# A second expert layer's row blocks are cut anew: seven late pairs, two single blocks and six small blocks in place of eight, one and five

## Chip, cores and metric

The kernel runs on one core of a Trainium2 chip. The metric is the device time in microseconds of one execution of the whole program. Three runs of the kernel before gave 780.1, 777.2 and 779.71 us; their median, 779.71 us, is the time that the change is measured against.

## What is computed

Three layers follow each other, all in float32. The first is a gated linear attention with complex decay over 4 x 8 heads of 768 steps and 48 channels, the second a layer of 3072 rows with a maximum over three products. The third, which the change touches, is a layer with eight experts of which each row takes one:

```python
xn = x / (np.linalg.norm(x, axis=-1, keepdims=True) + 1e-06)
en = expert_emb / (np.linalg.norm(expert_emb, axis=-1, keepdims=True) + 1e-06)
logits = xn @ en.T / tau
expert_idx = np.argmax(logits, axis=1)
...
gate_w = probs[np.arange(N), expert_idx]
for e in range(E):
    mask = expert_idx == e
    h = np.maximum(x[mask] @ w1[e], 0.0)
    out[mask] = gate_w[mask, None] * (h @ w2[e])
```

There are N = 3072 rows of 384, and an expert has a hidden width of 1024. On the inputs drawn here the eight experts take 1305, 521, 427, 153, 107, 15, 14 and 530 rows; of the first 2816 rows 1199 go to expert 0, and no other expert has 512 of them.

## The kernel before

**Stages.** `phase1` (L1073 on) computes the attention and the first dense layer. Its instructions go through a `Recorder`, which plans their order on each engine from written-out costs and then issues them, so that they all carry line L368. At its end `route_early` (L1011) routes the first 22 tiles of 128 rows. `phase2` (L1418) is the expert layer; its instructions carry their own lines, and the order on each engine is set by the scheduler of the tile framework from modelled times.

**Blocks of rows.** Rows of one expert are gathered from the DRAM tensor `x1d` by indirect loads into blocks of 128 (`gather`, L1264), and a block's result is scattered to `out` in the same manner (L1358). There are three kinds of step:
- A pair is two blocks, 256 rows, of one expert. Its products are made of float32r halves: weights and rows are split into a high and a low part and three products are added. The first product takes 72 matmuls (L1336), the second 24 for each block (L1352).
- A single is one block. Its first product is plain float32 (`ph<-xT,w1s` in the trace, 48 records), its second is as in a pair.
- A small block, or mini (`small`, L1362), holds up to MT = 32 rows of one expert. It loads its expert's two weights for itself (`w1m` and `w2m`, 1.5 MB each, one buffer each), and its few matmuls (`pxm`, `phm`, `pt`, `pym`, `psm`) are placed between those of one step and the next.

**How rests are cut.** `late_route` (L1157) counts the rows of every expert, takes off the early pairs, and calls `pairs_of` with a least of 129: a rest of 129 to 256 rows is a pair with empty places. What is then left is a mini if it has up to 32 rows, else single blocks. With the counts above that is: four early pairs of expert 0; eight late pairs (one of expert 0, two of 1, two of 2, one of 3, two of 7); one single (expert 4); five minis (experts 0, 1, 5, 6, 7).

**Order.** `STEPS` lists the steps. Steps 0 and 1 are the first early pair taken as two singles, then come the pairs 2 to 6, the single as step 7, and the pairs 8 to 13. `WITH = 5, 7, 9, 11, 12` are the steps with a mini. Seven further single steps (`SPARE`) are run by `last_blocks` only if the counts need them. In step k the program gathers the rows of step k + 2, loads the weights of step k + 1 (skipped on the chip by `cond` if the expert stays), and splits those weights on ScalarE and VectorE (`prep`, L1288 to L1298). The next mini's first weight and its rows (`xgm`, L1373) are asked for in the step ahead of it; its second weight at its step's start. At most four row buffers (`xg`, `xgm`) live at once.

**Gates.** In both routes `slots` (L968) writes a one-hot table of blocks, multiplied by row number and by three bfloat16 parts of each row's gate (L982 to L991), and `place` (L994) multiplies it on TensorE with one-hot positions. `join` (L1002) adds the parts up, so that `gate_of` holds the gate of every place; the results' last step (`yo`, L1356; `ym`, L1412) multiplies by it. `late_route` runs beside steps 1 to 3.

The lines that set the cut:

```python
TE, PE, PL, SG = 22, 4, 8, E
KE, KP = 2 * PE, 2 * (PE + PL)
NBLK = KP + SG
MT, MINI = 32, 5
SPARE = 7
STEPS = steps("ppppp" "s" "pppppp")
WITH = 5, 7, 9, 11, 12
```

Of the kernel before, what the change touches and what calls it, by code (L numbers as in the profile page):

```python
# [9 lines left out]
F32 = mybir.dt.float32  # L10
F32R = mybir.dt.float32r
BF16 = mybir.dt.bfloat16
# [24 lines left out]

TE, PE, PL, SG = 22, 4, 8, E
KE, KP = 2 * PE, 2 * (PE + PL)
NBLK = KP + SG  # L40
MT, MINI = 32, 5

SPARE = 7


def steps(order):

    out, p, s = [(0, 1), (1, 1)], 2, KP
    for c in order:
        out.append((p, 2) if c == "p" else (s, 1))  # L50
        p, s = (p + 2, s) if c == "p" else (p, s + 1)
    assert (p, s) == (KP, NBLK - SPARE)
    return out + [(i, 1) for i in range(s, NBLK)]


STEPS = steps("ppppp" "s" "pppppp")

WITH = 5, 7, 9, 11, 12
NE, NS = 1 + PE, len(STEPS)

# [322 lines left out]
class Prog:  # L383
# [6 lines left out]
    def consts(self, pool):  # L390
# [46 lines left out]
        self.dst = pool.tile([128, NBLK + MINI - KE], I32, name="dstrow")  # L437
        self.gate_of = pool.tile([128, NBLK + MINI], F32, name="slotgate")

# [515 lines left out]
    def pairs_of(self, new, cnt, T, n, least, name):  # L955

        v = self.q.vector

        k256 = self.k128[:, 1 + (least == 256):min(T + 1, NTILE):2]
        gt, num, tk = new([E, k256.shape[1]], name + "gt"), new([E], name + "n"), new([E], name + "t")  # L960
        v.tensor_tensor(gt, bc(cnt, 2, k256.shape[1]), bc(k256, 1, E), op=ALU.is_ge if least == 256 else ALU.is_gt)
        v.tensor_reduce(num, gt, axis=AX.X, op=ALU.add)
        st, end = self.sums(new, num, name)
        v.tensor_scalar_min(tk, st, float(n))
        v.scalar_tensor_tensor(tk, end, float(n), tk, op0=ALU.min, op1=ALU.subtract)
        return num, st, end, tk

    def slots(self, new, slot1, T, k):  # L968

        v = self.q.vector  # L970
        v.tensor_mul(slot1, slot1, self.oh[:, :, :T])
        slot = new([T], "slot")
        v.tensor_reduce(slot, slot1.rearrange("p e t -> p t e"), axis=AX.X, op=ALU.add)
        v.tensor_scalar_add(slot, slot, -1.0)
        si, pb = new([3, T], "sloti", I32), new([2, T], "posblk")
        v.tensor_copy(si[:, 0], slot)
        v.tensor_scalar(si[:, 1], si[:, 0], 127, None, op0=ALU.bitwise_and)
        v.tensor_scalar(si[:, 2], si[:, 0], 7, None, op0=ALU.arith_shift_right)
        v.tensor_copy(pb, si[:, 1:])

        g, r, gp = self.gates[:, :T], new([T], "grest"), new([T, 4], "gparts", BF16)
        for i in range(3):  # L982
            v.tensor_copy(gp[:, :, i], g)
            if i < 2:
                v.tensor_sub(r, g, gp[:, :, i])
                g = r
        ohb, val = new([T, k], "ohb", BF16), new([T, 5, k], "ohval", BF16)
        v.tensor_tensor(ohb, bc(self.blk[:, :k], 1, T), bc(pb[:, 1], 2, k), op=ALU.is_equal)
        v.tensor_mul(val[:, :, 0], ohb, bc(self.k128[:, :T], 2, k))
        v.tensor_scalar(val[:, :, 1], ohb, self.row1, None, op0=ALU.mult)  # L990
        v.tensor_mul(val[:, :, 2:], bc(ohb, 2, 3), bc(gp[:, :, :3], 3, k))  # L991
        return pb[:, 0], val
# [8 lines left out]

    def join(self, tok, gate, ps):  # L1002
        v = self.q.vector
        ps = ps.rearrange("p (a k) -> p a k", a=5)
        v.tensor_copy(tok, ps[:, 0])
        v.tensor_add(tok, ps[:, 1], tok)
        v.tensor_copy(gate, ps[:, 2])
        for i in (3, 4):
            v.tensor_add(gate, ps[:, i], gate)

    def route_early(self):  # L1011
# [36 lines left out]
        v.scalar_tensor_tensor(rank, rank, 1.0, ok, op0=ALU.add, op1=ALU.mult)  # L1048
        at, val = self.slots(new, rank, T, N)
        ps = self.tl(self.pg, [128, 5 * N], "g", 2, "slots0")  # L1050
# [5 lines left out]
        tok = new([N], "tok")  # L1056
        self.join(tok, self.gate_of[:, :N], ps)
        v.tensor_scalar_add(self.src[:, :N], tok, -1.0)
# [98 lines left out]
    def late_route(self, pool, pg):  # L1157
# [18 lines left out]
        v.tensor_scalar(left, rank, 0.0, None, op0=ALU.is_ge)  # L1176
        _, st, end, tk = self.pairs_of(new, cnt, T, PL, 129, "mid")
        v.tensor_copy(ends[:, 0], end)
# [11 lines left out]
        few, bm = new([E], "few"), new([MINI, E], "bem")  # L1190
        v.tensor_scalar(few, cnt, float(MT), None, op0=ALU.is_le)
        v.tensor_mul(few, few, nb)
        stm, endm = self.sums(new, few, "few")
# [20 lines left out]

        v.tensor_scalar(stm, stm, 128.0, 1.0 + 128 * (NBLK - KE), op0=ALU.mult, op1=ALU.add)
        v.tensor_sub(stm, stm, base[:, 1])
        v.tensor_mul(stm, stm, few)
        v.tensor_add(base[:, 1], base[:, 1], stm)
        s2 = new([E, T], "slot2")
        v.tensor_add(s2, rank, bc(base[:, 1], 2, T))  # L1220
        v.scalar_tensor_tensor(s2, rank, 0.0, s2, op0=ALU.is_ge, op1=ALU.mult)
        v.tensor_add(slot, slot, s2)
        v.tensor_mul(slot, slot, left)
        self.gate(new, lg, mx, self.gates[:, late])
        yield
        at, val = self.slots(new, slot, T, N)
        ps = pg.tile([128, 5 * N], F32, tag="rt", bufs=1, name="slots")
        for t0 in range(0, T, 6):
# [3 lines left out]
        tok, e0 = new([N], "tok"), new([2, N], "empty")  # L1232
        self.join(tok, self.gate_of[:, KE:], ps)
        v.tensor_scalar(e0[:, 0], tok, 1.0, 0.0, op0=ALU.subtract, op1=ALU.max)
# [7 lines left out]
    def moe2(self, pool, wq, pg, regs, q1, q2):  # L1242
# [21 lines left out]
        def gather(i, n):  # L1264
            for i in range(i, i + n):
                xg = pool.tile([128, DM], F32, tag="xg", bufs=4, name=f"xg{i}")
                g.indirect_dma_start(out=xg, out_offset=None, in_=self.x1d[:TE * 128] if i < KE else self.x1d,
                                     in_offset=bass.IndirectOffsetOnAxis(ap=self.src[:, i:i + 1], axis=0),
                                     bounds_check=(TE * 128 if i < KE else NT) - 1, oob_is_err=False)
                st["x", i] = xg  # L1270

        def prep(i, n):
# [71 lines left out]
        def mm2(i, n, b):  # L1344
            py = pg.tile([128, DM], F32, tag="py", bufs=2, name=f"py{i}_{b}")
            w2, o, m = st["w2", i], 0, 4 // n
            r = slice(b * 128, (b + 1) * 128)
            for k in range(KF):
                (hi, lo), (wh, wl) = st["h", i, k // 4, k % 4 // m], w2[k // 4]
                f = k % m  # L1350
                for a, c in ((hi, wh), (hi, wl), (lo, wh)):
                    t.matmul(py, a[:, f, r], c[:, k % 4], start=o == 0, stop=o == 3 * KF - 1)  # L1352
                    o += 1
            i += b
            y = pool.tile([128, DM], F32, tag="yo", bufs=3, name=f"yo{i}")
            s.activation(y, py, AF.Copy, scale=self.gate_of[:, i:i + 1])  # L1356
            row = self.src[:, i:i + 1] if i < KE else self.dst[:, i - KE:i - KE + 1]
            g.indirect_dma_start(out=self.io["out"], in_=y, in_offset=None,  # L1358
                                 out_offset=bass.IndirectOffsetOnAxis(ap=row, axis=0), bounds_check=NT - 1, oob_is_err=False)
        return load, gather, prep, share, transpose, mm1, mm2, st  # L1360

    def small(self, pool, mp, pg, m):  # L1362
# [11 lines left out]
                             in_offset=bass.IndirectOffsetOnAxis(ap=self.src[:, i:i + 1], axis=0),  # L1374
                             bounds_check=NT - 1, oob_is_err=False)
        yield

# [33 lines left out]
        y = pool.tile([128, DM], F32, tag="yo", bufs=3, name=f"ym{m}")  # L1411
        s.activation(y, ps, AF.Copy, scale=self.gate_of[:, i:i + 1])  # L1412
        g.indirect_dma_start(out=self.io["out"], in_=y, in_offset=None,
# [85 lines left out]
    def run(self):  # L1499
        tc = self.tc  # L1500
        with ExitStack() as ctx:
# [6 lines left out]
            self.x1d = dp.tile([NT, DM], F32, name="x1d")  # L1508
            self.xd = dp.tile([NT, DM], F32, name="xd")
            self.phase1()  # L1510
            self.phase2()
# [38 lines left out]
    def last_blocks(self):  # L1550
# [3 lines left out]
        with self.tc.tile_pool(name="lb", bufs=1) as p, self.tc.tile_pool(name="lbg", bufs=1, space=PSUM) as pg, \  # L1554
# [6 lines left out]
            nc.sync.dma_start(dst, self.dst[:, bass.ds(k + (i0 - KE), 1)])  # L1561
            nc.sync.dma_start(gate, self.gate_of[:, bass.ds(k + i0, 1)])
            e = nc.values_load(tab[0:1, :], engines=[ET.SP], min_val=0, max_val=E - 1,
                               skip_runtime_bounds_check_because="a count of 8 comparisons, of which one fails")
            w1 = p.tile([128, 3, FF2], F32, name="lb_w1")
            w2 = p.tile([128, FF2 // 128, DM], F32, name="lb_w2")
# [220 lines left out]
```

## Time and profile before

| | us |
|---|---|
| median of three runs (777.2 to 780.1) | 779.71 |
| profiled execution, device time | 777.83 |
| its span, first to last instruction | 775.9 |
| TensorE busy with matmuls | 719.6 (93% of the span) |
| VectorE busy | 607.1 (78%) |
| ScalarE busy | 441.5 (57%) |
| GpSimd busy | 104.6 (13%) |

The span leaves 1.9 us of the device time outside it. Matmuls are pipelined, so TensorE counts as busy almost without a break where nothing stops it; what a step costs there is read from the distance between the starts of its first and the next step's first matmul. "Idle before" is the time in which an engine had nothing running ahead of an instruction, with what ended it. The granted clock is given as a share of full speed.

### The profile page before, as it was taken

To read this page: it belongs to the slowest core of one execution; us is meant where nothing else is said; L and a number is where in the kernel's file an instruction comes from. 1 tells how busy PE (TensorE), PEld (TensorE's weight loads), DVE (VectorE), ACT (ScalarE), POOL (GpSimd) and SP (SyncE) were. 2 spreads that over 40 slices of the span, in tenths; PEclk is the share of its full clock that TensorE was granted. 3 is DMA by queue.
4 is the path that set the end of the run, shared out by engine and by line. 5 is a ranking of instruction groups with operands and counts; after the bars stand their busy time and mean duration, and the time that the engine had idled before them with its cause. 6 is when DMAs were issued, how large, how long until landed. Compare 5 with 4: busy or idle time off the path is not lost. (4 is left out here: it accounts for less than half of the span.)

```text
span 775.9 us, 18425 instructions
## 1 busy us (share of the span) xinstructions
PE 719.6 (93%) x7318; PEld 657.1 (85%) x7318; DVE 607.1 (78%) x1211; ACT 441.5 (57%) x1007; POOL 104.6 (13%) x156
## 2 busy tenths in 40 slices
PE   0568989999999999999999999999999999999995
PEld 0447679899899989888998988989989898999985
DVE  8999799999999999999999722869986455546420
ACT  8997485656667555757455442167535466544521
POOL 6301000000000000000000000022122223324211
PEclk9987899999999999999999999999999999999999
DMA  8608062635345380834516240051058775691500
GB/s 330 263 21 197 1 174 69 139 131 137 106 105 119 91 209 13 197 99 119 137 37 140 60 86 22 13 233 42 22 236 335 283 299 213 210 368 49 186 22 26
DMA packets 28753, 107.42 MB, mean 138 GB/s; under 512 B 5061, under 2 KB 8180, under 8 KB 25569
## 3 DMA queue, kind: packets, MB, share of 16 engines
q1 hardware_dynamic: 20432, 77.55, 33.5%
q0 software_dynamic: 7952, 28.21, 11.3%
q8 instruction: 59, 0.97, 0.5%
q10 hardware_dynamic: 272, 0.39, 0.1%
q14 instruction: 38, 0.30, 0.1%
HBM read 96.35 MB, written 10.62 MB: 138 GB/s over the span
## 5 line engine op out<-in xcount | busy, mean ns | idle before, releaser
L368 PE MATMUL ph<-xhi,w 128*128 128x256 f32 x864 | 134.0, 291 | 0.9 <-ACT xhi L368 0.9
L368 PEld LDWEIGHTS ph<-xhi,w 128*128 128x128 f32 x864 | 114.3, 191 | 8.3 <-issue 4.7
L1298 DVE TENSOR_TENSOR w2l<-queue_q_buf,w2h 128x768 fp32r<-128x768 f32 x52 | 47.9, 954 | 39.1 <-ACT w2h L1297 39.0
L1336 PE MATMUL ph<-xh,w1s 128*128 128x256 f32 x264 | 77.0, 292 | 0.0
L368 PE MATMUL ph<-xlo,w 128*128 128x256 f32 x432 | 75.3, 283 | 0.4 <-DVE xlo L368 0.4
L1336 PE MATMUL ph<-xh,w1l 128*128 128x256 f32 x264 | 74.6, 283 | 0.0
L1336 PE MATMUL ph<-xl,w1s 128*128 128x256 f32 x264 | 74.6, 283 | 0.0
L1352 PE MATMUL py<-w2h,hlo 128*128 128x384 f32 x200 | 67.9, 340 | 1.8 <-DVE hlo L1341 1.8
L1352 PE MATMUL py<-w2h,hhi 128*128 128x384 f32 x200 | 69.1, 345 | 0.0
L1352 PE MATMUL py<-w2l,hhi 128*128 128x384 f32 x200 | 67.6, 338 | 0.0
L368 PEld LDWEIGHTS ph<-xlo,w 128*128 128x128 f32 x432 | 62.0, 191 | 0.6 <-DVE xlo L368 0.6
L368 POOL DMA_DIRECT2D v<-v x24 | 12.9, 538 | 365.4 <-PE py L368 364.5
L1341 DVE SCALAR_TENSOR_TENSOR hlo<-ph,hhi 128x512 fp32r<-128x512 f32 x50 | 34.3, 688 | 30.0 <-ACT hhi L1340 30.0
L1340 ACT ACTIVATE hhi<-ph 128x512 fp32r<-128x512 f32 x50 | 29.9, 598 | 49.0 <-PE ph L1336 48.8
L368 PE MATMUL pa<-S 112*128 112x128 f32 x384 | 51.7, 279 | 2.2 <-DVE at L368 1.7
L1336 PEld LDWEIGHTS ph<-xh,w1s 128*128 128x128 f32 x264 | 50.5, 191 | 3.8 <-issue 3.1
L368 PEld LDWEIGHTS pa<-S 112*128 112x128 f32 x384 | 48.2, 193 | 4.5 <-DVE at L368 2.9
L1297 ACT CAST w2h<-queue_q_buf 128x768 fp32r x52 | 40.8, 833 | 18.1 <-PE py L1352 16.7
L1336 PEld LDWEIGHTS ph<-xh,w1l 128*128 128x128 f32 x264 | 50.5, 191 | 0.5
L1336 PEld LDWEIGHTS ph<-xl,w1s 128*128 128x128 f32 x264 | 50.5, 191 | 0.0
L368 DVE TENSOR_TENSOR sa<-X 128x384 f32<-128x384 f32 x84 | 46.5, 554 | 0.7
L1292 DVE TENSOR_TENSOR w1l<-queue_q_buf,w1s 128x1536 fp32r<-128x1536 f32 x22 | 38.6, 1759 | 9.3 <-PE ph L1336 7.4
(399 smaller groups left out, 1809.1 us busy)
## 6 DMA issues: line engine op xcount, KB each, us to landing
queue_q_buf<-w SPq DMA_DIRECT2D x26, 1536.0 KB
S<-QK SPq DMA_DIRECT2D x46, 289.1 KB
X<-a SPq DMA_DIRECT2D x11, 768.0 KB
QKr<-qk SPq DMA_DIRECT2D x11, 768.0 KB
w1m<-w SPq DMA_DIRECT2D x5, 1536.0 KB
w2m<-w SPq DMA_DIRECT2D x5, 1536.0 KB
v<-v POOLq DMA_DIRECT2D x24, 224.0 KB, 3.6
r<-w POOLq DMA_DIRECT2D x12, 384.0 KB, 8.4
```

What stands on the lines that cost most here:

```text
L368: getattr(getattr(self.nc, c[0]), c[1])(*c[2], **c[3])
L1292: v.tensor_sub(wl[k], av.rearrange("p (a b) -> p a b", b=FF2)[:, :, c], w1[k].bitcast(F32))
L1297: s.copy(hi, b[:, c])
L1298: v.tensor_sub(lo, bv[:, c], hi.bitcast(F32))
L1336: t.matmul(ph[:, f], a, b, start=o == 0, stop=o == len(ops) - 1)
L1340: s.activation(hi, ph, AF.Relu).ins,
L1341: v.scalar_tensor_tensor(lo, ph, 0.0, hi.bitcast(F32), op0=ALU.max, op1=ALU.subtract).ins]
L1352: t.matmul(py, a[:, f, r], c[:, k % 4], start=o == 0, stop=o == 3 * KF - 1)
```

## The change

The limit from which a rest becomes a pair is raised from 129 to 161 rows. Rests of 129 to 160 rows become one single block and one mini, for which `late_route` tells an expert's last, small block from its full ones (`s3`). With the counts above, expert 3's 153 rows are no longer a pair but a single of 128 and a mini of 25. There are seven late pairs, two singles (experts 3 and 4) and six minis. The singles are the last two steps, 12 and 13, and the minis lie in steps 6 to 11, all of them pairs.

The late gates are no longer placed by matmuls: all gates are turned by one transposition on TensorE, copied by ScalarE, and written to a DRAM tensor `gd`. For each late block and each mini the GpSimd queue issues one more indirect load, of 128 single gates, right behind that of its rows (`gate_rows`, six buffers). In `slots` the product with the row number in the tile moves from VectorE to ScalarE, in the early route too.

```diff
-TE, PE, PL, SG = 22, 4, 8, E
+TE, PE, PL, SG = 22, 4, 7, E + 2
-MT, MINI = 32, 5
-SPARE = 7
+MT, MINI = 32, 6
+SPARE = 8
-STEPS = steps("ppppp" "s" "pppppp")
-WITH = 5, 7, 9, 11, 12
+STEPS = steps("ppppppppppss")
+WITH = 6, 7, 8, 9, 10, 11
...
-    def slots(self, new, slot1, T, k):
+    def slots(self, new, slot1, T, k, parts):
...
-        g, r, gp = self.gates[:, :T], new([T], "grest"), new([T, 4], "gparts", BF16)
-        for i in range(3):
-            v.tensor_copy(gp[:, :, i], g)
-            if i < 2:
-                v.tensor_sub(r, g, gp[:, :, i])
-                g = r
-        ohb, val = new([T, k], "ohb", BF16), new([T, 5, k], "ohval", BF16)
+        ohb, val = new([T, k], "ohb", BF16), new([T, 2 + parts, k], "ohval", BF16)
         v.tensor_tensor(ohb, bc(self.blk[:, :k], 1, T), bc(pb[:, 1], 2, k), op=ALU.is_equal)
+        self.q.scalar.activation(val[:, :, 1], ohb, AF.Copy, scale=self.row1)
         v.tensor_mul(val[:, :, 0], ohb, bc(self.k128[:, :T], 2, k))
-        v.tensor_scalar(val[:, :, 1], ohb, self.row1, None, op0=ALU.mult)
-        v.tensor_mul(val[:, :, 2:], bc(ohb, 2, 3), bc(gp[:, :, :3], 3, k))
+        if parts:
...
-        _, st, end, tk = self.pairs_of(new, cnt, T, PL, 129, "mid")
+        _, st, end, tk = self.pairs_of(new, cnt, T, PL, 128 + MT + 1, "mid")
...
-        v.tensor_scalar(few, cnt, float(MT), None, op0=ALU.is_le)
-        v.tensor_mul(few, few, nb)
+        v.scalar_tensor_tensor(few, nb, -128.0, cnt, op0=ALU.mult, op1=ALU.add)
+        v.tensor_scalar(few, few, float(MT - 128), None, op0=ALU.is_le)
+        v.scalar_tensor_tensor(few, nb, 1.0, few, op0=ALU.min, op1=ALU.mult)
...
+        v.tensor_scalar_mul(nb, nb, 128.0)
         v.tensor_sub(stm, stm, base[:, 1])
+        v.tensor_sub(stm, stm, nb)
         v.tensor_mul(stm, stm, few)
-        v.tensor_add(base[:, 1], base[:, 1], stm)
-        s2 = new([E, T], "slot2")
-        v.tensor_add(s2, rank, bc(base[:, 1], 2, T))
+        s2, s3 = new([E, T], "slot2"), new([E, T], "slot3")
+        v.tensor_tensor(s3, rank, bc(nb, 2, T), op=ALU.is_ge)
+        v.tensor_mul(s3, s3, bc(stm, 2, T))
+        v.tensor_add(s3, s3, bc(base[:, 1], 2, T))
+        v.tensor_add(s2, s3, rank)
...
         self.gate(new, lg, mx, self.gates[:, late])
+        pt, rows = pg.tile([T, 128], F32, tag="rt", bufs=1, name="pgate"), pool.tile([T, 128], F32, name="grow")
+        t.transpose(pt, self.gates, self.ident)
+        self.q.scalar.copy(rows.rearrange("t (b l) -> t l b", l=L), pt.rearrange("t (l b) -> t l b", l=L))
+        self.q.sync.dma_start(self.gd.rearrange("(t p) a -> t (p a)", p=128), rows)
         yield
-        at, val = self.slots(new, slot, T, N)
-        ps = pg.tile([128, 5 * N], F32, tag="rt", bufs=1, name="slots")
+        at, val = self.slots(new, slot, T, N, 0)
+        ps = pg.tile([128, 2 * N], F32, tag="rt", bufs=1, name="slots")
...
-        self.join(tok, self.gate_of[:, KE:], ps)
+        self.join(tok, ps)
...
                 st["x", i] = xg
+                if i >= KE:
+                    st["gate", i] = self.gate_rows(pool, i)
...
-            s.activation(y, py, AF.Copy, scale=self.gate_of[:, i:i + 1])
+            s.activation(y, py, AF.Copy, scale=self.gate_of[:, i:i + 1] if i < KE else st.pop(("gate", i)))
...
+    def gate_rows(self, pool, i):
+
+        x = pool.tile([128, 1], F32, tag="grow", bufs=6, name=f"gate{i}")
+        self.nc.gpsimd.indirect_dma_start(out=x, out_offset=None, in_=self.gd,
+                                          in_offset=bass.IndirectOffsetOnAxis(ap=self.src[:, i:i + 1], axis=0),
+                                          bounds_check=NT - 1, oob_is_err=False)
+        return x
```

The mini's `small` calls `gate_rows` behind its own gather and scales `ym` by it. `join` leaves the gates out where none are given, `gate_of` keeps the eight early blocks only, `pairs_of` compares with the remainder of the least, and `last_blocks` loads its gates from `gd`.

## Rows read from the trace of the kernel before

**Rows 1.** The page: the span; VectorE and the granted clock in 40 slices.

```profile
span 775.9 us, 18425 instructions
...
DVE  8999799999999999999999722869986455546420
...
PEclk9987899999999999999999999999999999999999
```

**Rows 2.** Two windows: length, busy PE, PEld, DVE, ACT, POOL, clock, DMA share, GB/s.

```profile
534.93:576.66 41.73, 39.94 (x283) 38.82 (x282) 40.80 (x114) 19.79 (x28) 8.63 (x6) 0.96 0.20 77
594.05:768.04 173.99, 173.15 (x1313) 159.69 (x1312) 83.57 (x98) 85.00 (x130) 45.53 (x39) 1.00 0.51 192
```

**Rows 3.** Windows of four steps of the second MoE, same columns.

```profile
576.66:594.05 17.39, 17.39 (x126) 17.39 (x126) 9.80 (x13) 9.98 (x14) 5.08 (x5) 1.00 1.01 412
...
634.38:646.80 12.42, 12.42 (x108) 11.35 (x108) 6.21 (x9) 8.70 (x13) 5.04 (x5) 1.00 0.45 162
...
688.20:706.56 18.36, 18.36 (x133) 18.09 (x129) 9.87 (x12) 9.66 (x15) 5.06 (x5) 1.00 0.62 246
...
728.00:750.18 22.18, 22.18 (x177) 19.41 (x173) 10.93 (x13) 8.82 (x16) 3.28 (x4) 1.00 0.23 85
```

**Rows 4.** Groups of PE instructions by line and shape, 500 to 776 us.

```profile
L1336 PE MATMUL ph<-xT,w1s 128*128 128x128 f32 x144 | 16.7, 276 | 0.0
...
L1390 PE MATMUL phm<-w1m,xm 128*32 128x256 f32 x120 | 7.5, 383 | 0.0
...
L999 PE MATMUL slots<-ohval,ohpos 128*128 128x145 bf16 x24 | 2.3, 229 | 0.0
```

**Rows 5.** VectorE in order of time, 530 to 570 us: start, length, line.

```profile
536.96 0.27 DVE L983 CAST gparts<-gates 128x24 bf16<-128x24 f32 x1
...
545.37 0.17 DVE L1192 TENSOR_TENSOR few<-few,nblocks 128x8 f32<-128x8 f32 x1
...
551.90 0.36 DVE L1220 TENSOR_TENSOR slot<-incl,base 128x192 f32<-128x192 f32 x1
...
563.62 0.41 DVE L990 TENSOR_SCALAR ohval<-ohb,row 128x696 bf16<-128x696 bf16 x1
563.93 2.33 DVE L991 TENSOR_TENSOR ohval<-ohb,gparts 128x2088 bf16<-128x2088 bf16 x1
```

**Rows 6.** TensorE in order of time, 568 to 573 us.

```profile
568.92 0.57 PE L999 MATMUL slots<-ohval,ohpos 128*128 128x145 bf16 x6
571.28 0.44 PE L1352 MATMUL py<-w2h,hlo 128*128 128x384 f32 x1 [1.79 <-DVE hlo L1341]
...
572.50 0.52 PE L1352 MATMUL py<-w2l,hhi 128*128 128x384 f32 x1
```

**Rows 7.** GpSimd queue in order of time, 590 to 592 us.

```profile
590.08 1.00 POOL L1358 DMA_INDIRECT out<-yo,srcrow  x1 [10.85 <-DMA out<-yo,srcrow]
591.38 1.04 POOL L1373 DMA_INDIRECT xgm<-x1d,srcrow  x1 [0.30 <-issue]
```

**Rows 8.** TensorE in order of time, 597 to 600 us.

```profile
599.35 0.34 PE L1383 MATMUL pxm<-ident,xgm 32*128 32x32 f32 x3 [0.84 <-DMA xgm<-x1d,srcrow]
```

**Rows 9.** GpSimd queue in order of time, 718 to 728 us.

```profile
718.01 1.02 POOL L1373 DMA_INDIRECT xgm<-x1d,srcrow  x1 [4.40 <-PE pxg L1313]
...
727.59 1.00 POOL L1358 DMA_INDIRECT out<-yo,dstrow  x1 [2.63 <-ACT yo L1356]
```

**Rows 10.** TensorE in order of time, 733 to 734 us.

```profile
733.14 0.37 PE L1383 MATMUL pxm<-ident,xgm 32*128 32x32 f32 x3
```

**Rows 11.** Instructions that touch xgm: GpSimd durations min/median/max, DMA to landing.

```profile
L1373 POOL DMA_INDIRECT xgm<-x1d,srcrow x5: 998/1040/1992, 591.4 to 718.0; - x5
...
DMA to landing us min/median/max: 3.8/8.7/10.3
```

**Rows 12.** Instructions that touch xg, 500 to 777 us.

```profile
L1267 POOL DMA_INDIRECT xg<-x1d,srcrow x24: 994/1022/2558, 503.8 to 711.6; - x24
```

**Rows 13.** One wait of TensorE over the span: total us, times, longest.

```profile
PE pk L368 <- DMA S<-QK: 2.1, 2, 1.6
```

More of the change, by code (lines that the diff above doesn't have):

```diff
@@ L437, in consts @@
         self.dst = pool.tile([128, NBLK + MINI - KE], I32, name="dstrow")
-        self.gate_of = pool.tile([128, NBLK + MINI], F32, name="slotgate")
+        self.gate_of = pool.tile([128, KE], F32, name="slotgate")
         self.mtab = pool.tile([128, MINI], I32, name="mtab")
@@ L960, in pairs_of @@
         gt, num, tk = new([E, k256.shape[1]], name + "gt"), new([E], name + "n"), new([E], name + "t")
-        v.tensor_tensor(gt, bc(cnt, 2, k256.shape[1]), bc(k256, 1, E), op=ALU.is_ge if least == 256 else ALU.is_gt)
+        v.scalar_tensor_tensor(gt, bc(cnt, 2, k256.shape[1]), float(least % 128), bc(k256, 1, E), op0=ALU.subtract,
+                               op1=ALU.is_ge)
         v.tensor_reduce(num, gt, axis=AX.X, op=ALU.add)
@@ L979, in slots @@
         v.tensor_copy(pb, si[:, 1:])
-        g, r, gp = self.gates[:, :T], new([T], "grest"), new([T, 4], "gparts", BF16)
-        for i in range(3):
-            v.tensor_copy(gp[:, :, i], g)
-            if i < 2:
-                v.tensor_sub(r, g, gp[:, :, i])
-                g = r
-        ohb, val = new([T, k], "ohb", BF16), new([T, 5, k], "ohval", BF16)
+        ohb, val = new([T, k], "ohb", BF16), new([T, 2 + parts, k], "ohval", BF16)
         v.tensor_tensor(ohb, bc(self.blk[:, :k], 1, T), bc(pb[:, 1], 2, k), op=ALU.is_equal)
+        self.q.scalar.activation(val[:, :, 1], ohb, AF.Copy, scale=self.row1)
         v.tensor_mul(val[:, :, 0], ohb, bc(self.k128[:, :T], 2, k))
-        v.tensor_scalar(val[:, :, 1], ohb, self.row1, None, op0=ALU.mult)
-        v.tensor_mul(val[:, :, 2:], bc(ohb, 2, 3), bc(gp[:, :, :3], 3, k))
+        if parts:
+            g, r, gp = self.gates[:, :T], new([T], "grest"), new([T, 4], "gparts", BF16)
+            for i in range(3):
+                v.tensor_copy(gp[:, :, i], g)
+                if i < 2:
+                    v.tensor_sub(r, g, gp[:, :, i])
+                    g = r
+            v.tensor_mul(val[:, :, 2:], bc(ohb, 2, 3), bc(gp[:, :, :3], 3, k))
         return pb[:, 0], val
@@ L1000, in place, with join @@
                                      stop=t0 + k == T - 1)
-    def join(self, tok, gate, ps):
+    def join(self, tok, ps, gate=None):
         v = self.q.vector
-        ps = ps.rearrange("p (a k) -> p a k", a=5)
+        ps = ps.rearrange("p (a k) -> p a k", k=tok.shape[1])
         v.tensor_copy(tok, ps[:, 0])
         v.tensor_add(tok, ps[:, 1], tok)
+        if gate is None:
+            return
         v.tensor_copy(gate, ps[:, 2])
@@ L1048, in route_early @@
         v.scalar_tensor_tensor(rank, rank, 1.0, ok, op0=ALU.add, op1=ALU.mult)
-        at, val = self.slots(new, rank, T, N)
+        at, val = self.slots(new, rank, T, N, 3)
         ps = self.tl(self.pg, [128, 5 * N], "g", 2, "slots0")
@@ L1056, in route_early @@
         tok = new([N], "tok")
-        self.join(tok, self.gate_of[:, :N], ps)
+        self.join(tok, ps, self.gate_of)
         v.tensor_scalar_add(self.src[:, :N], tok, -1.0)
@@ L1375, in small @@
                              bounds_check=NT - 1, oob_is_err=False)
+        gate = self.gate_rows(pool, i)
         yield
@@ L1411, in small @@
         y = pool.tile([128, DM], F32, tag="yo", bufs=3, name=f"ym{m}")
-        s.activation(y, ps, AF.Copy, scale=self.gate_of[:, i:i + 1])
+        s.activation(y, ps, AF.Copy, scale=gate)
         g.indirect_dma_start(out=self.io["out"], in_=y, in_offset=None,
@@ L1509, in run @@
             self.xd = dp.tile([NT, DM], F32, name="xd")
+            self.gd = dp.tile([NT, 1], F32, name="gd")
             self.phase1()
@@ L1561, in last_blocks @@
             nc.sync.dma_start(dst, self.dst[:, bass.ds(k + (i0 - KE), 1)])
-            nc.sync.dma_start(gate, self.gate_of[:, bass.ds(k + i0, 1)])
             e = nc.values_load(tab[0:1, :], engines=[ET.SP], min_val=0, max_val=E - 1,
                                skip_runtime_bounds_check_because="a count of 8 comparisons, of which one fails")
+            nc.gpsimd.indirect_dma_start(out=gate, out_offset=None, in_=self.gd,
+                                         in_offset=bass.IndirectOffsetOnAxis(ap=src, axis=0),
+                                         bounds_check=NT - 1, oob_is_err=False)
             w1 = p.tile([128, 3, FF2], F32, name="lb_w1")
```

## The prediction, made before the change ran

> **What bounds the kernel now.** I read the page first [rows 1]: VectorE is near full only in the first half and around two thirds of the span, and TensorE has its full clock but for the start and one later dip. The change touches the expert layer, so I cut its stretch into windows [rows 2]. Two things are to be seen. From 594 us to the last matmul TensorE is busy 173.15 of 173.99 us, VectorE 83.57, ScalarE 85.00, GpSimd 45.53, and the DMA has a share of 0.51: there every matmul taken out is time gained. In the 41.73 us from 534.93 on VectorE is busy 40.80, TensorE idles 1.79 us, and the mean clock is 0.96: there VectorE, which carries the late routing beside the splitting of weights, sets the pace. Windows of single steps [rows 3] then give the prices.
>
> **The exchange of blocks.** A pair goes; a single and a mini come.
> - The pair: the window from 688.20 holds one without a mini, 18.36 us, but also the sum of the mini before it. That from 576.66 has none, 17.39 us, but starts two of its 126 matmul records late, so 17.7. I take 17.9, between the two.
> - The mini: the window from 728.00 is a pair and a mini right behind another mini, as all but the first will be: 22.18 us. Less 17.9 that is 4.3, with ends of 22.18 - 18.36 = 3.8 and 22.18 - 17.7 = 4.5.
> - The single: its window has 12.42 us [rows 3], with a mini's first product (7.5 us for five, 1.5) and its transpositions (0.3) in it [rows 4, 10], so 10.6. That still has a pair's six transpositions where it needs three; I take 10.4, with ends of 10.1 and 10.6. Its own first product is 16.7/3 = 5.6 us of it [rows 4].
>
> That makes -17.9 + 10.4 + 4.3 = **-3.2 us**, and -4.4 or -2.6 at the ends. All of it lies on TensorE's path.
>
> **Weights.** Before, the steps change experts to 0, 1, 4, 1, 2, 3, 7: seven loads, and five minis load for themselves. Afterwards it is six and six. The bytes stay, at a DMA share of 0.51 [rows 2], so I cost this at nothing. The mini's first weight has one buffer and waits on the sync queue for the mini ahead of it to finish its first product; behind that wait stands the load of the next step's weights, which still has most of a step to land.
>
> **The late routing.** Out of VectorE's work go the product with three gate parts, 2.33 us, that with the row number, 0.41, five operations that make the gate parts at 0.17 to 0.27 each (1.0), and three adds and copies of the gates at about 0.17 (0.5): 4.2 us [rows 5]. In come three operations on 192 elements at 0.36 and, net, two small ones at 0.17, 1.4 us [rows 5]. So 2.8 us less in a stretch that VectorE fills. The stop of 1.79 us, in which TensorE waits for `hlo`, and the slow matmuls behind it (0.32 us from start to start at half clock) lie at its end [rows 6]. By VectorE alone, with its idle 0.93 us kept, the stretch falls by 2.8; without that idle by 3.7. TensorE would allow more: 1.79 of idling, 0.04 x 41.73 = 1.7 of clock, and most of the placing matmuls, whose 145 columns become 60 (2.3 us [rows 4]). I take the smaller engine's figure, **-2.8 us**. The other end is a loss. The transposition of the gates is new in TensorE's queue, which runs in order, and the two steps' products stand behind it; the trace shows no such wait, so I bound it by the one on VectorE that it has there, and at worst get +1.8 instead.
>
> ScalarE takes the product with the row number and a copy of 24 rows; it is busy 19.79 of 41.73 us [rows 2], so nothing. The write of `gd` goes on the sync queue some 35 us before the first gate is loaded: the gates are read at 536.96 [rows 5], and the first late rows are asked for after the routing ends. The sync queue's next real work behind it is the weights of step 6. Nothing either.
>
> **The first mini** waits 0.84 us for its rows [rows 8]. These were asked for late: the scatter ahead in GpSimd's queue had stood 10.85 us behind the landing of the scatter before it [rows 7], in a window in which the DMA ran full at 412 GB/s [rows 3]. This mini moves one step back, out of that crowd: **-0.8 us**, at least nothing. For the five that now follow each other, the one such case shows no idle time [rows 10], so I add nothing; the other end is 0.84 each, 4.2.
>
> **Gate loads.** Sixteen blocks and six minis bring 22 more issues on GpSimd's queue. At the median of 1.02 us and 0.30 between [rows 12, 7] a step with a mini has nine issues, 11.9 us of its 22.2, and all run beside TensorE: nothing. If that cover goes, see the rivals.
>
> **The two singles at the end.** In step 12 ScalarE must split the weights of step 13. In the single's window it was busy 8.70 us with a pair's split and a mini [rows 3], and 10.4 are there: nothing. The last scatter and what follows it stay.
>
> **The attention stage** is planned again, because an operation of the early route changes its engine and price. No row shows what another order costs; I take nothing, and as bounds the longest kind of wait on the DMA in its steady part, 2.1 us either way [rows 13].
>
> **Sum:** -3.2 - 2.8 - 0.8 = -6.8 us. The profiled execution's 777.83 would become 771.0. It lies 1.9 us below the median of the three runs, which the result is set against, so I forecast 779.71 - 6.8 = **772.9 us**.
>
> **Rivals.**
> 1. *Only the exchange counts.* VectorE's gain is eaten by another order of the routing, or by the wait for the gates, and the following minis get their rows late. Against it speaks that VectorE is busy 98% of that stretch, for it that the scheduler goes by modelled times and let `hlo` come late before. That gives 779.71 - 3.2 = 776.5, and up to 4.2 more if each mini waits as the first did: around 777.5, within half a percent.
> 2. *Slower: the gates hold the minis' rows in the queue.* Gates have six buffers. With two blocks each for steps k, k + 1 and k + 2 and a mini, a seventh is asked for, and then GpSimd waits for step k's result to be scaled. If `xgm` stands behind that, its issue moves from 718.01 to after the second result, whose scatter went at 727.59 [rows 9]: with the gate's own issue to 728.9. It lands 8.7 us later [rows 11], at 737.6, where TensorE wants it at 733.14 [rows 10]: 4.5 us late for each of five minis, 22 us, so 795. It decides the outcome when the rows come over 2 us late each, that is when the second and not the first result is waited for. Against it: the scheduler sets an instruction in the queue when its model has it ready, and `xgm` stood there early, waiting 4.40 us for its buffer [rows 9].
> 3. *Slower: the issues themselves grow long.* The longest issue for `xg` took 2.56 us against a median of 1.02 [rows 12]. If all did, nine a step would be 9 x (2.56 + 0.30) = 25.7 us against 22.2 of TensorE, and GpSimd would bound steps 6 to 11: +3.5 x 6 = 21 us, 794. The median speaks against it, and so does GpSimd's load of 45.53 in 174 us [rows 2]. The Trainium skill has a cause for such issues (SBUF — State Buffer, "SBUF: two separate sides"): descriptors of DMAs from GpSimd's queue can't be written while certain VectorE operations hold the port pair that both share. The trace agrees that a few issues stretch, and not that most do.
> 4. *It doesn't do what it says.* If a block were left over, `last_blocks` would run eight trips, each with 3 MB of weights, 7.6 us at 412 GB/s, so over 60 us. The counts speak against it: 281, 521, 427 and 530 rows make 1 + 2 + 2 + 2 = 7 pairs, 153 and 107 two singles, and rests of 25, 9, 25, 15, 14 and 18 six minis.
>
> **How the numbers follow.** Half a percent, 3.9 us, is about what a measurement of this kernel can tell from no change, so faster means below 775.8. I give the forecast 0.63, the first rival 0.27, the second 0.06, the third 0.03 and the last 0.01. The forecast's own range is 769 to 776. Its low end is the best of the exchange and of VectorE (-4.4 - 3.7 - 0.8 = -8.9) from the profiled execution's time; 768.5 leaves a little for the attention's new plan. The first rival reaches to 780. So the range is 768.5 to 780.0: it leaves out the slower rivals and little more.
>
> **What would show it.** Right: eleven pair steps become ten, with two singles of about 10.4 us at the end. The two steps from the routing's start take 39 instead of 41.7 us, no wait for `hlo` over 0.5 us is left, and the clock stays full there. All `pxm` have no idle time ahead. GpSimd has 22 more issues of about 1 us. Wrong: a wait on `pgate` or on `xgm`; result copies (`yo`, `ym`) that wait for a gate's landing; a stop in step 12 or 13 on weights; or an expert layer that starts over 2 us earlier or later than now.

## The result: the changed kernel is half a percent slower

The changed kernel takes 783.09 us (median of five, 782.46 to 783.93) against 779.71 us; the runs of the two kernels don't overlap. The ratio of the two is estimated at 1.0061, with a 95% interval of 1.0045 to 1.0078; the two medians alone give 1.0043. Forecast were 772.9 us and a range that ended at 780.0. The profiled execution took 782.46 us, with this span on its page:

```profile
span 780.2 us, 18462 instructions
```

Windows of steps of the changed kernel come first (length; busy PE, PEld, DVE, ACT, POOL with instructions; clock; DMA share; GB/s). The first line answers to the first of [rows 2], the second and the last to the pair and the single of [rows 3].

```profile
536.10:574.20 38.10, 36.84 (x281) 35.93 (x280) 36.93 (x104) 21.12 (x30) 3.67 (x4) 1.00 0.26 98
591.70:609.20 17.50, 17.50 (x127) 17.50 (x126) 10.58 (x13) 10.08 (x14) 9.70 (x9) 1.00 0.26 78
...
630.60:656.00 25.40, 23.81 (x177) 20.90 (x173) 10.65 (x13) 14.55 (x21) 11.95 (x10) 0.93 0.63 244
656.00:678.10 22.10, 22.10 (x177) 19.33 (x173) 10.95 (x13) 8.23 (x15) 9.45 (x9) 1.00 0.70 241
678.10:702.90 24.80, 22.70 (x178) 19.49 (x174) 10.65 (x13) 14.55 (x21) 12.43 (x10) 1.00 0.65 250
702.90:725.00 22.10, 22.10 (x178) 19.33 (x174) 10.93 (x13) 8.23 (x15) 8.37 (x8) 1.00 0.66 248
725.00:749.90 24.90, 22.31 (x174) 19.14 (x170) 8.30 (x11) 16.19 (x24) 4.55 (x5) 1.00 0.65 269
749.90:760.60 10.70, 10.70 (x82) 10.42 (x79) 3.21 (x4) 3.30 (x7) 1.55 (x2) 1.00 0.07 23
```

Two steps with a mini, 8 and 10, run without a break and take 22.1 us. Three of the same kind, 7, 9 and 11, take 2.6 to 3.4 us more (25.5, 24.7 and 24.9). The waits of TensorE and of ScalarE from 590 us to the last matmul (total us, times, longest) say who stops whom:

```profile
PE psm L1434 <- ACT part L1431: 4.5, 3, 1.7
PE ph L1351 <- DVE hlo L1356: 1.8, 2, 0.9
```

```profile
ACT w1s L1303 <- DMA queue_q_buf<-w: 25.2, 4, 7.5
```

In the kernel before TensorE had one stop in that stretch, 0.84 us [rows 8], and no split of a weight waited for the DMA. Step 7 of the changed kernel shows the chain: the sync queue, ScalarE and TensorE in order of time (start, length, line, what, idle time ahead and what ended it).

```profile
619.84 0.34 SPq L1394 DMA_DIRECT2D w1m<-w  x1
621.51 0.34 SPq L1274 DMA_DIRECT2D queue_q_buf<-w  x1
622.18 0.33 SPq L1275 DMA_DIRECT2D queue_q_buf<-w  x1
```

```profile
624.86 0.58 ACT L1371 ACTIVATE yo<-py,gate 128x384 f32<-128x384 f32 x1 [3.36 <-PE py L1367]
632.81 2.85 ACT L1303 CAST w1s<-queue_q_buf 128x1536 fp32r x2 [7.37 <-DMA queue_q_buf<-w]
635.57 0.57 ACT L1371 ACTIVATE yo<-py,gate 128x384 f32<-128x384 f32 x1
636.04 0.47 ACT L1431 COPY part<-pym 128x384 f32<-128x384 f32 x1
```

```profile
629.80 0.83 PE L1429 MATMUL pym<-w2m,hT 128*32 128x384 f32 x8
...
636.65 0.88 PE L1434 MATMUL psm<-part,mask 128*128 128x384 f32 x2 [1.59 <-ACT part L1431]
...
637.77 0.46 PE L1351 MATMUL ph<-xh,w1s 128*128 128x256 f32 x1
638.02 0.42 PE L1351 MATMUL ph<-xh,w1l 128*128 128x256 f32 x1
```

The weights for step 8 are issued at 621.51, behind the mini's `w1m`, which had to wait for the mini ahead. ScalarE comes to their split at 625.44 and waits until 632.81. In ScalarE's order that split, due only for step 8, stands ahead of the second `yo` of step 6 and of `part`, the copy of its mini's product `pym`, which was ready soon after 630. So `part` is 5 us late, TensorE stops for it, and the matmuls behind the stop start 0.21 us apart instead of 0.12 for 3.4 us, at a granted clock of 0.5, which is 1.2 GHz (0.93 as the window's mean). The same happens for the weights of steps 10 and 12.

The span against that of before, by stretches (from the start of a stretch's first matmul to that of the next one's):

| stretch | before | after | difference |
|---|---|---|---|
| up to the expert layer | 514.2 | 514.9 | +0.8 |
| steps 0 to 4, with the late routing | 79.9 | 76.8 | -3.1 |
| step 5 to the last matmul | 174.0 | 178.7 | +4.7 |
| behind the last matmul | 7.9 | 9.8 | +1.9 |

The sum is +4.3, the difference of the spans. The attention's code is the same in this kernel and in those of experiments 1, 4, 5 and 8, and there the first stretch is 513.5 to 516.2 us long: the 0.8 us lie within that scatter.

### The profile page after: what moved, and what is told of

The parts are those of the page before. It is cut to its first block, busy times and chain, and to the rows that moved or that the text cites. A ratio compares the mean times of both kernels' runs of the same rounds, so it can differ in the third digit from the quotient of the medians.

```text
span 780.2 us, 18462 instructions
## 1 busy us (share of the span) xinstructions
PE 716.0 (92%) x7315; PEld 648.9 (83%) x7315; DVE 598.4 (77%) x1200; ACT 441.5 (57%) x1010; POOL 130.9 (17%) x179
## 5 line engine op out<-in xcount | busy, mean ns | idle before, releaser
L1351 PE MATMUL ph<-xh,w1s 128*128 128x256 f32 x240 | 69.4, 289 | 1.8 <-DVE hlo L1356 1.8
L1351 PE MATMUL ph<-xl,w1s 128*128 128x256 f32 x240 | 67.8, 282 | 0.0
L1351 PE MATMUL ph<-xh,w1l 128*128 128x256 f32 x240 | 67.7, 282 | 0.0
L1367 PE MATMUL py<-w2h,hhi 128*128 128x384 f32 x192 | 66.4, 346 | 0.0
L1367 PE MATMUL py<-w2h,hlo 128*128 128x384 f32 x192 | 64.8, 337 | 0.0
L1367 PE MATMUL py<-w2l,hhi 128*128 128x384 f32 x192 | 64.7, 337 | 0.0
L1351 PEld LDWEIGHTS ph<-xh,w1s 128*128 128x128 f32 x240 | 45.7, 191 | 5.6 <-issue 3.1
L1351 PEld LDWEIGHTS ph<-xl,w1s 128*128 128x128 f32 x240 | 45.9, 191 | 0.0
L1351 PEld LDWEIGHTS ph<-xh,w1l 128*128 128x128 f32 x240 | 45.8, 191 | 0.0
L368 DVE TENSOR_TENSOR m<-X,C 128x768 f32<-128x768 f32 x48 | 44.3, 949 | 1.0 <-ACT C L368 0.8
```

The costliest lines, as they stand in the source:

```text
L368: getattr(getattr(self.nc, c[0]), c[1])(*c[2], **c[3])
L1351: t.matmul(ph[:, f], a, b, start=o == 0, stop=o == len(ops) - 1)
```

## Experiments

The theories, by the letters that the expectations give them. Q: the sync queue's wait for the mini holds the weights back, and their lateness is the loss. A, formed after the first four runs: lateness does no harm by itself; the harm is where the scheduler put ScalarE's split. G: the gate loads do it. B: the bytes of a step's weights and a mini's together are too much for one step. Each run stands beside runs of the kernel before on its chip: 778.04 us in the first four, 778.48 for the next four, 778.91 for the last two.

**1. `w1m` behind the step's weights.** The mini's first weight is asked for one stage later, so behind the next step's weights on the sync queue.

```diff
-        w1 = mp.tile([128, KD, FF2], F32, tag="w1m", ...)
-        nc.sync.dma_start(w1, ...)
         xg = pool.tile([128, DM], F32, tag="xg", ...)
...
         yield
+        w1 = mp.tile([128, KD, FF2], F32, tag="w1m", ...)
+        nc.sync.dma_start(w1, ...)
         w2 = mp.tile([128, KF, DM], F32, tag="w2m", ...)
```

> The changed kernel with one move: a mini's first weight is asked for behind the loads of the next step's weights on the sync queue, not ahead of them; same bytes, same buffers. Theory Q (order on the sync queue: the step's weights stand behind the wait of w1m for the mini before): the three stops in steps 7, 9 and 11 (6.3 us of TensorE idle and 1.7 us of slow clock after the first) go, 783.1 becomes about 775 (773 to 777). Rival B (bytes: a step's and a mini's weights together are too much for one step): unchanged, 783. Rival G (the gate loads on the GpSimd queue hold things up): unchanged, 783.

781.41 us, ratio 1.0042 (1.0027 to 1.0056). The stops in steps 7, 9 and 11 are gone, but step 8 now takes 26.4 us and step 10 24.1. Its ScalarE, in order of time:

```profile
658.86 0.23 ACT L1409 COPY xm<-pxm 128x96 f32<-128x96 f32 x1
667.63 1.47 ACT L1303 CAST w1s<-queue_q_buf 128x1536 fp32r x1 [8.54 <-DMA queue_q_buf<-w]
669.01 1.08 ACT L1355 ACTIVATE hhi<-ph 128x512 fp32r<-128x512 f32 x2
```

The weights of step 10 now went out at 655.52, 2.3 us into step 8 and not 13.5 us as in the changed kernel, but the scheduler had put their split earlier too, ahead of the `hhi` for which TensorE stopped 2.21 us, with half-clock matmuls behind that stop. Moving the load moved the stop. Q alone doesn't explain that.

**2. The gate loads alone.** The changed kernel with before's cut and order.

```diff
-TE, PE, PL, SG = 22, 4, 7, E + 2
+TE, PE, PL, SG = 22, 4, 8, E
-MT, MINI = 32, 6
-SPARE = 8
+MT, MINI = 32, 5
+SPARE = 7
-STEPS = steps("ppppppppppss")
-WITH = 6, 7, 8, 9, 10, 11
+STEPS = steps("ppppp" "s" "pppppp")
+WITH = 5, 7, 9, 11, 12
-        _, st, end, tk = self.pairs_of(new, cnt, T, PL, 128 + MT + 1, "mid")
+        _, st, end, tk = self.pairs_of(new, cnt, T, PL, 129, "mid")
```

> The kernel before with the late gates by indirect loads alone; eight pairs, one single and five minis as before. Q and B: the late routing's two steps fall by about 3.2 us, the start of the expert layer comes 0.8 us later and the end after the last matmul is 1.9 us longer, as in the changed kernel: 779.7 becomes 779 (777.5 to 780.5), with no stop on the copy of part. G: stops of the changed kernel's kind appear here, 783 or more.

782.83 us, ratio 1.0059 (1.0041 to 1.0077). No stop for `part`. The late routing's two steps gain 3.9 us where 3.2 was expected. The loss lies in step 4, 25.1 us where before had 17.4 [rows 3]: 4.6 us of stops, and a granted clock of 0.86 over the step. TensorE in order of time:

```profile
584.75 0.55 PE L1328 MATMUL pxg<-ident,xg 128*128 128x128 f32 x3 [1.97 <-DMA xg<-x1d,srcrow]
587.96 0.90 PE L1328 MATMUL pxg<-ident,xg 128*128 128x128 f32 x3 [2.66 <-DMA xg<-x1d,srcrow]
588.51 0.67 PE L1367 MATMUL py<-w2h,hhi 128*128 128x384 f32 x1
```

A scatter now stands ahead of the gathers and a gate load between them, so the second block's rows for step 5 are asked for at 578.41; before it was 573.93. The first mini's two weights and the next step's load in the same stretch (DMA share 0.99), and the rows come late. The changed kernel asks for them as late, at 578.58, but loads less in that stretch (DMA share 0.71), and doesn't stop.

**3. The new cut alone.** The kernel before with the lines of the cut (those above, turned round, and the routing of the last small block). Gates are placed by matmuls, and VectorE keeps all that it had; against the changed kernel:

```diff
-                if i >= KE:
-                    st["gate", i] = self.gate_rows(pool, i)
...
-        at, val = self.slots(new, slot, T, N, 0)
-        ps = pg.tile([128, 2 * N], F32, tag="rt", bufs=1, name="slots")
+        at, val = self.slots(new, slot, T, N)
+        ps = pg.tile([128, 5 * N], F32, tag="rt", bufs=1, name="slots")
```

> The kernel before with the new cut alone (seven pairs, two singles last, six minis in steps 6 to 11), gates placed by matmuls as before. Q and B: the three stops are there without a gate load, -4 us for the exchange and the first mini's wait, +8 us of stops and slow clock, and the late routing gains nothing: 783 to 785. G: no stops, 775 to 776.

781.15 us, ratio 1.0035 (1.0019 to 1.0052), with the changed kernel's waits:

```profile
PE psm L1416 <- ACT part L1413: 4.3, 3, 1.8
PE ph L1342 <- DVE hlo L1347: 1.3, 2, 0.7
```

So the stops come with the cut, and G is out. The late routing gained as well, 2.1 us, which had been forecast at nothing. Behind its last matmul lie 7.9 us, as before; in all kernels with 22 gate loads 9.7 to 9.9.

**4. The minis apart.**

```diff
-WITH = 6, 7, 8, 9, 10, 11
+WITH = 5, 6, 8, 9, 10, 12
```

> The changed kernel with the minis in steps 5, 6, 8, 9, 10 and 12. Q: a stop comes where two minis lie in the two steps ahead of a change of expert (steps 8, 10, 12); only 8 and 9 ahead of step 10 do, so one stop, in step 9, of 1.2 to 2.5 us in place of 6.3: about 778 (776 to 780). B: steps 7, 9 and 11 with a step's weights and, in step 9, a mini's: one to two stops, 778 to 781. G: 783.

788.87 us, ratio 1.0139 (1.0118 to 1.0161), a miss: one stop for `part` is left, in step 9 (1.71 us), as Q had it, but the first mini is back in step 5 and brings experiment 2's waits for rows (5.6 us), and steps 6 and 10 get stops for `hhi` and `hlo`. Neither of the two choices of places that were run with gate loads and six minis is free of such waits by itself.

**5. The split behind the running step's relu.** The changed kernel with one edge of order on ScalarE; no load is moved.

```diff
-                next(p, 0)
+                if k < WITH[0]:
+                    next(p, 0)
                 if k == 0:
                     transpose(*STEPS[1])
                 if k != 1:
                     mm1(i, n, 0)
+                if k >= WITH[0]:
+                    with tc.issue_after(st["last"][0]):
+                        next(p, 0)
```

> The changed kernel, with one order edge: from step 6 on, ScalarE's split of the next step's first weight may be issued only behind the first `hhi` of the step that is running. Nothing is loaded earlier or later on purpose. Theory A (ScalarE's queue): in the changed kernel the scheduler put that split ahead of the running step's `part` and `hhi`, where it waited up to 7.5 us for its weight; the load may be as late as it is, the harm is that finished products stand behind the wait. It expects the three stops ahead of `psm` (1.59, 1.23, 1.67 us) and the two on `hlo` (0.87, 0.92) to go, with the half-clock stretch of 3.4 us, steps 7, 9 and 11 near 22.1 instead of 25.48, 24.73, 24.94, no wait of a split for its weight over 2 us, and 783.1 - 8.2 = 775 us. Theory Q (the weight is simply too late, whatever stands behind it): the wait moves to the next step's first product, which then stops for `w1s`, and the time stays within 2 us of 783.

772.03 us (771.16 to 772.1), ratio 0.9921 (0.9906 to 0.9936); 775 were expected. No stop of TensorE over 0.25 us is left behind step 2. Step 7 of this kernel, the sync queue and then ScalarE in order of time; then its window and the next one:

```profile
618.45 0.34 SPq L1394 DMA_DIRECT2D w1m<-w  x1
620.11 0.34 SPq L1274 DMA_DIRECT2D queue_q_buf<-w  x1
```

```profile
629.37 0.48 ACT L1431 COPY part<-pym 128x384 f32<-128x384 f32 x1 [0.87 <-PE pym L1429]
...
633.73 0.60 ACT L1355 ACTIVATE hhi<-ph 128x512 fp32r<-128x512 f32 x1 [1.52 <-PE ph L1351]
634.22 1.47 ACT L1303 CAST w1s<-queue_q_buf 128x1536 fp32r x1
```

```profile
629.20:651.30 22.10, 22.10 (x178) 19.33 (x174) 11.02 (x13) 11.13 (x18) 10.23 (x10) 1.00 0.71 279
651.30:673.40 22.10, 22.10 (x178) 19.33 (x174) 11.05 (x13) 11.13 (x18) 10.06 (x10) 1.00 0.71 240
```

The weights go out 9.1 us ahead of step 7, as in the changed kernel (621.51 against 630.56); those of steps 10 and 12 go out 13.5 us into step 8 and 13.0 into step 10 in both. They are as late as they were; but `part` and `hhi` now stand ahead of the split, which finds its weights there. A holds, and Q falls.

**6. The same edge on the new cut alone** (experiment 3 and the lines of 5).

> The new cut without the gate loads, with the same order edge on ScalarE's split. Theory A expects its stops (1.82, 1.46, 0.98, 0.57, 0.69 us) to go with the half-clock stretch, so about 5.5 + 1.7 = 7.2 us less than the new cut alone (span 778.6): a span of 771.5, and about 774 us where the kernel before has 778 to 780. The tail stays at 7.9 us. Theory Q expects 780 to 782. Against the changed kernel with that edge it tells what the gate loads are worth as a whole: by the tails 1.9 us worse with them, by the late routing's stretch 1.0 better.

770.67 us (769.34 to 770.8), ratio 0.9898 (0.9883 to 0.9914): faster than both kernels of the change, without the gate loads, and 1.4 us below experiment 5 on the same chip. Forecast were about 774.

**7. Six gate loads.** Experiment 3 with `gd` written, and loads for the minis' gates alone.

```diff
+        gate = self.gate_rows(pool, i)
...
-        s.activation(y, ps, AF.Copy, scale=self.gate_of[:, i:i + 1])
+        s.activation(y, ps, AF.Copy, scale=gate)
```

> The new cut, with gates by placing matmuls for all blocks and by indirect loads for the six small blocks alone (6 instead of 22 gate loads). The tail (last matmul to the end of the span) was 7.9 us with none and 9.7 to 9.9 with 22; GpSimd's closing drain was 1.29 and 3.09 us. If the drain grows with the number of gate loads (theory N), it is 1.29 + 1.80 x 6 / 22 = 1.8 us and the tail 8.4. If any use of such a load brings it (theory U), it is 3.1 and 9.8. If it hangs on what was issued last, a scatter in all of them, it stays 1.29 and 7.9. Time about 781.

One run, 779.6 us. GpSimd's closing drain takes 1.78 us, what N gives. The tail is 7.9 us all the same, and not N's 8.4: other parts of it vary by as much.

**8. Minis with few bytes.** Five minis reload 8 columns of each weight and compute with the first mini's others.

```diff
-        w1 = mp.tile([128, KD, FF2], F32, tag="w1m", ...)
-        nc.sync.dma_start(w1, ...)
+        if m == 0:
+            self.w1m = mp.tile([128, KD, FF2], F32, tag="w1m", ...)
+        w1, c = self.w1m, FF2 if m == 0 else 8
+        nc.sync.dma_start(w1[:, :, :c], ...[:, :, :c])
```

> The changed kernel, in which only the first small block loads its two weights whole; the other five load 8 columns of each (24 to 64 KB instead of 1.5 MB), behind the same waits on the sync queue, and multiply by what is left of the first one's: those small blocks' results are left wrong in the remaining columns' part. It tells the two ends of why the weights for steps 8, 10 and 12 land late. Theory W (the wait on the sync queue): they are issued behind the small block's wait, about 9 us ahead of the step that needs them split, so the bytes don't matter: ScalarE's waits stay at 5 us or more and the stops at 4 us or more in all; time above 781. Theory B (the bytes ahead and beside them on the DMA): without 1.57 MB ahead, at some 410 GB/s 3.8 us, the weight lands about 4 us earlier and the waits fall from 7.4 to about 3.5 us, the stops ahead of `psm` go but for 0.3 us, and the time is about 776.

772.94 us, ratio 0.9941 (0.9922 to 0.9961). The split still waits for its weights three times, 4.4 us at most (7.5 before), and nothing stops. That is B's direction, and W's time of over 781 did not come, but it doesn't part the two: with the shorter loads the scheduler also placed the mini's loads and the splits elsewhere. How much of the lateness is bytes and how much the queue stays open; by experiment 5 it decides nothing.

**9. The control: the edge on the kernel before** (the lines of 5).

> The control: the kernel before, uncut, with the same order edge on ScalarE's split from its first small block on (step 5). In the kernel before no split waits on the DMA in those steps and no product of theirs stops for ScalarE. If theory A is right, the edge does nothing by itself there: 776 to 780 us, the ratio within half a percent of 1, and what it gave the changed kernel (783.1 to 772.0) is the removal of the stops that the change had made. If the edge is a gain in any kernel (theory E), before falls as well, by up to the 11 us, and the change itself remains worth nothing.

778.77 us, ratio 0.9997 (0.9978 to 1.0016). The edge gains nothing where no split waits; what it gives the changed kernel is what the change had put in.

**10. Six scatters fewer.** Experiment 6 without the minis' scatters.

```diff
         s.activation(y, ps, AF.Copy, scale=self.gate_of[:, i:i + 1])
-        g.indirect_dma_start(out=self.io["out"], in_=y, ...)
```

> The new cut with the edge and without gate loads, in which the six small blocks' results are not written out (their six scatters are left out; the output lacks their rows). GpSimd's closing drain was 1.29 us with none, 1.78 with 6 and 3.09 with 22 gate loads, 0.082 us for each. If it goes by the number of indirect DMAs of any kind, six fewer make it 1.29 - 0.49 = 0.8 us; if by something that the gate loads alone have (their 4-byte rows, their loads on top of the others), it stays at 1.29. The span is 769.0 less at most a microsecond.

One run, 771.4 us. The drain takes 0.80 us, so scatters count in it as gate loads do.

## Why the prediction was wrong

Experiment 5 is the changed kernel without the stops, so it shows which terms held (both spans from one execution each; the forecast is the sum's):

| term | forecast | changed kernel | with the edge |
|---|---|---|---|
| exchange of blocks and first mini's wait, with weights at nothing | -3.2 - 0.8 + 0 | +4.7 | -4.6 |
| late routing (steps 0 to 4) | -2.8 | -3.1 | -3.0 |
| attention stage | 0 | +0.8 | -0.7 |
| last scatter and what follows | 0 | +1.9 | +1.8 |
| sum | -6.8 | +4.3 | -6.5 |

**The step that failed is "Weights".** It read "I cost this at nothing", since the bytes stay, and of the load behind the mini's wait, that it "still has most of a step to land". Both halves were about bytes and TensorE. For TensorE they held: step 8's weights were there at 632.81, 23 us ahead of that step. But the first to read them is ScalarE, whose instructions run in order here, and which came to the split at 625.44, 31 us ahead of step 8. The prediction named what is queued behind the wait on the sync queue and stopped there. It didn't ask what is queued behind the instruction that waits for that load. That term, taken at nothing, measures 4.7 + 4.6 = 9.3 us: 6.3 us of stops over 0.25 us, and 2.9 us more in which TensorE counts as busy (23.81, 22.70 and 22.31 us in steps 7, 9 and 11 against 22.10, 22.10 and 21.70). Of these, 1.7 are the half-clock matmuls in step 7; the 1.2 in steps 9 and 11 came at full clock.

**Exchange and first mini: right.** With the edge the stretch gains 4.6 where 4.0 was forecast. A pair takes 17.5 us (17.9 was taken), a mini 22.1 - 17.5 = 4.6 (4.3), the two singles 10.7 and 9.7 (10.4 each). The first mini's rows come in time. Minis right behind each other don't idle for rows.

**Late routing: right size, reason not shown.** The step put the 2.8 us down to 2.8 us less work on VectorE. In steps 0 to 4 VectorE is busy 67.0 us in the changed kernel and was 68.7 before, so 1.7 us less. Each half of the change alone shortens the routing's two steps as much as both do (41.73 us before, 38.10 after): first the gate loads with the cut of before (experiment 2), then the new cut with all of VectorE's work (experiment 3):

```profile
536.20:574.10 37.90, 36.64 (x281) 35.79 (x280) 36.87 (x105) 21.06 (x30) 3.89 (x4) 1.00 0.09 30
535.70:573.20 37.50, 37.11 (x273) 36.33 (x272) 37.35 (x101) 20.00 (x29) 4.62 (x4) 1.00 0.25 90
```

So the half that takes work off VectorE was enough for it, and so was the half that doesn't. VectorE in order of time, with the new cut alone and then before:

```profile
565.12 0.68 DVE L1347 SCALAR_TENSOR_TENSOR hlo<-ph,hhi 128x512 fp32r<-128x512 f32 x1
...
568.53 2.40 DVE L992 TENSOR_TENSOR ohval<-ohb,gparts 128x2160 bf16<-128x2160 bf16 x1
```

```profile
570.55 0.68 DVE L1341 SCALAR_TENSOR_TENSOR hlo<-ph,hhi 128x512 fp32r<-128x512 f32 x1
...
572.03 0.68 DVE L1341 SCALAR_TENSOR_TENSOR hlo<-ph,hhi 128x512 fp32r<-128x512 f32 x1
```

With the new cut the last `hlo` of step 3 stands ahead of the products with the gate parts; in the kernel before that step's last two stood behind them [rows 5, 6]. There another order on VectorE took away the stop of 1.79 us and the slow matmuls behind it, with no work gone. Over steps 0 to 4 the new cut alone gains 2.1 of the 3.1 us, and the gate loads on top of it 1.1. The transposition of the gates did add a wait of TensorE on VectorE, 1.26 us, a sign of being wrong that the prediction had named, and the start of the routing one of 0.66; both lie within the 3.1.

**"The last scatter and what follows it stay": wrong**, by 1.9 us. With 22 more indirect DMAs GpSimd's closing work is longer (below).

**Rivals.** The second named a real wait: gate loads stood 36.9 us behind `yo`, ten times. But no `xgm` came late for it. The loss that did come was of another kind, an in-order wait on ScalarE, which no rival had.

## What to carry to other kernels

When a load comes later, follow it to the first instruction that reads it, and ask what stands behind that instruction on its own in-order queue: late data cost nothing here once finished products were put ahead of the split. A scheduler that goes by modelled times can undo a gain of 6 us by one copy that it puts too early, so look at waits on the DMA on every engine after each change of order, and try an order edge before moving loads. Gates by many small loads bought 1.4 us in steps 0 to 4 and cost 1.9 at the end of the kernel (experiment 5 against 6).

## What the runs showed of the hardware

GpSimd's closing drain grows with the number of indirect DMAs that the program issued, by 0.082 us for each, over all twelve traces; gate loads and scatters count alike. The semaphore instruction ahead of it grows too. Each of these DMAs moves up to 128 rows, so whether it goes by DMAs or by rows is not shown.

| indirect DMAs | kernels | drain, us | semaphore instruction, us |
|---|---|---|---|
| 54 | experiment 10 | 0.80 | 0.38 |
| 60 | before, experiments 3, 6, 9 | 1.29 | 0.50 |
| 66 | experiment 7 | 1.78 | 0.62 |
| 82 | after, experiments 1, 2, 4, 5, 8 | 3.09 | 0.94 |

Together the two grow by 2.2 us for 22 gate loads. The whole stretch behind the last matmul varies in its other parts: it is 7.8 to 8.6 us with 60 indirect DMAs and 9.7 to 9.9 with 82, 1.8 us more at the median.

Not each stop of TensorE is followed by slow matmuls. Behind stops of 1.59 us (changed kernel, step 7), 1.82 (experiment 3) and 1.37 (experiment 4) the granted clock fell to 0.5, which is 1.2 GHz; behind stops of 1.67 us (changed kernel, step 11) and 2.14 (experiment 7) it stayed at 1.00. The stop's length alone doesn't tell it.
